# Fewer TensorE tiling changes, two weight loads swapped, and batch-1 transposes moved ahead of the last scale rows, in a one-core MM-DiT block

## The chip, the cores and the metric

The kernel runs on one core of one Trainium2 chip. The metric is the device time of one execution in microseconds (us). Before the change it was 120.38 us (three runs, 120.31 to 120.49). Two lengths occur below. The **time** is what the device reports for an execution. The **span** is what the trace covers, from the first to the last recorded instruction of the core.

## The reference

A joint attention block with image and text tokens (2 batches, 256 image and 32 text tokens, width D = 1152, bf16). Cut to what matters:

```python
mod_i = (silu(c) @ wmod_img).reshape(B, 6, 1, D)          # rows: shift, scale, gate, ... for the image
mod_t = (silu(c) @ wmod_txt).reshape(B, 6, 1, D)          # the same for the text
hi = layernorm(x_img) * (1 + sci) + shi                   # image tokens, scaled and shifted
ht = layernorm(x_txt) * (1 + sct) + sht
qi, ki, vi = split(hi @ wqkv_img);  qt, kt, vt = split(ht @ wqkv_txt)
q, k, v = concat(qt, qi), concat(kt, ki), concat(vt, vi)  # per batch: 32 text + 256 image tokens
a = softmax(q @ k.T * D ** -0.5) @ v
out_i = x_img + gai * (a[:, Nt:] @ wo_img)
out_t = x_txt + gat * (a[:, :Nt] @ wo_txt)
```

## The kernel before: the parts that the change touches

Twelve weight blocks of 1152 x 1152 pass through five SBUF slots. The loads of one queue are issued in order, and a load into a slot waits until the last reader of what was in it is done.

```python
w_sc_t = load_w(1, wmod_txt, D)            # text scale weights, slot 1
w_q_t = load_w(2, wqkv_txt, 0)
w_k_t = load_w(3, wqkv_txt, D)
w_v_t = load_w(1, wqkv_txt, 2 * D)         # text values: slot 1, after the text scale weights
w_ga_i = load_w(0, wmod_img, 2 * D)        # image gate: slot 0
w_ga_t = load_w(2, wmod_txt, 2 * D)
w_o_i = load_rows(3, wo_img, 0)
w_o_t = load_rows(1, wo_txt, 0)
```

A product with the two conditioning rows is made with four column tiles of 32 (tiling 128*32, set by `tile_position`), nearly all other large matmuls of the body with the full array (128*128); the text values and a few transposes have tilings of their own. In the head, the image scale rows end in one PSUM tile of 288 columns, which VectorE transposes at once, scales the first image columns with, and so opens the value matmuls:

```python
def mod_cols_of(gps, name):                # one VectorE transpose of [128, 9 x 32]
    t = const.tile([P, KT, LW], f32, ...)
    pin(nc.vector.transpose(t[:].rearrange("p c l -> p (c l)"), gps[:].rearrange("p c l -> p (c l)")))
    return t
...
sc_rows(0, 4)
warm_up(3)
sc_rows(4, 7)
warm_up(1)
out01 = x_transposes(0, 1)                 # six batch-1 transposes of 128x128
sc_rows(7, K8)
sc_rows(K8, KT)                            # the last scale rows to arrive
out31 = x_transposes(3, 1)
sc1_i = mod_cols_of(sc_ps, "scc")
out01()
x_scale(0, 3, 0)
out61 = x_transposes(6, 1)
v_open(A0, 0, 3)                           # the value matmuls begin
```

The places where the tiling changes in the body, the text rows, the scores, the softmax transposes and the text values:

```python
def txt_transposes():                      # nine transposes in 64-row tiling
    tpt = ps_tr.tile([P, KT, NTT], bf, tag="tr")
    for kt in range(KT):
        tr(tpt[:, kt, :], xn_t[:, kt * P:(kt + 1) * P], ident[0:NTT, 0:NTT])
    nc.scalar.copy(xT_t[:], tpt[:])
...
qk_img(w_k_i, 1, {1: (txt_shift_split, txt_rows_scale,),
                  6: (txt_rows_shift, txt_cols_shift, txt_modulate),
                  8: (lambda: qk_txt(0, w_q_t),)})
...
def attn_pair(ids0, ids1):                 # six full tiles of three feature blocks, cut
    ...
    for n, key in enumerate([x for pair in zip(t0, t1) for x in pair]):
        first = key in t1
        r0, (b, dt) = 64 * (n % 2), key    # two row tiles of 64
        mm((t1 if first else t0)[key][:], lhsT=v_t[r0:r0 + 64, dt * P:(dt + 1) * P],
           rhs=pTs[b][r0:r0 + 64, 2, :], start=first, stop=not first, tile_position=(r0, 0))
    ...
scores_txt()                               # 32-column tiles
scores_img(0)                              # full tiles
img_gate()                                 # 32-column tiles
scores_img(1)
v_txt()
p_transposes(0)                            # per batch: six full and three 32x32 transposes
txt_gate()
G = [[(b, dt) for dt in range(d0, d0 + 3)] for b in range(B) for d0 in range(0, KT, 3)]
attn_pair(G[0], G[1])
p_transposes(1)
attn_pair(G[2], G[3])
attn_pair(G[4], G[5])
```

## Time and profile before

| | before |
|---|---|
| time, median (range) of 4 runs | 120.34 us (120.27 to 120.49) |
| span of the profiled run | 118.6 us |
| time minus span | 1.8 us |
| TensorE (PE) busy | 112.1 us, 95% |
| first value matmul | 14.76 us |
| from there to the end of the span | 103.85 us |

The page of the profiled run gives busy time for each engine. The chain of waits follows the work that ended last back to the start, and names at each step what released it. In the chain a line is: start in us, length in us, engine, tile, source line, number of instructions. Line 61 is the helper through which every matmul goes, line 64 the one for transposes, so one has to go by the tile's name: `vps` are the image values, `gps` rows of scale, shift or gate, `sps` scores, `aps` attention, `pT_ps` softmax transposes, `ps` the other projections.

The prediction shows the head of this chain. Its part from 54 us on, cut, is what parts 3 to 6 of the change are about:

```profile
55.03 1.22 PE gps L61 x36
...
66.07 0.60 PE gps L61 x16
...
77.33 3.14 PE sps L61 x36
80.47 1.22 PE gps L61 x36
...
86.57 0.61 PE pT_ps L64 x9
...
90.55 0.50 PE pT_ps L64 x9
91.05 4.38 PE aps L61 x36
```

The text scale rows (36 `gps`) and shift rows (16 `gps`) are 11 us apart. The scores of text and of batch 0 are one entry of 36 matmuls and the image gate's 36 rows follow; the text scores come first there, so the 128*32 stays on both sides of the image scores are separate. The softmax transposes are in two places. No step in this stretch names another engine or a load: PE runs from one group to the next.

### The profile page before, as it was taken

How to read it: one execution, taken by the hardware profiler on the slowest of the kernel's cores; microseconds unless marked ns; L12 is line 12 of the kernel's file. 1: busy time of each engine (PE TensorE's matmuls, PEld its weight loads, DVE VectorE, ACT ScalarE, POOL GpSimd, SP SyncE). 2: the span in 40 equal slices, each digit the busy share in tenths (PEclk: the TensorE clock that was granted, in tenths of full speed). 3: DMA queues.
4: the chain of work that ended last, by engine and by line, in shares of the span. 5: the costliest groups of instructions: out<-in, count | busy, mean ns of one | idle time of the engine just before them, and what ended most of it. 6: DMA issues, size and time to landing. Idle time of an engine off the chain costs nothing.

```text
span 118.6 us, 2515 instructions
## 1 busy us (share of the span) xinstructions
PE 112.1 (95%) x1051; PEld 64.0 (54%) x1059; DVE 75.3 (63%) x157; ACT 41.8 (35%) x86; POOL 10.3 (9%) x31
## 2 busy tenths in 40 slices
PE   4988899999999999999999999999999999999990
PEld 1335544445674444445444457877876666666660
DVE  2568592063966799999999540048685666666571
ACT  4799620041752524323039233345327620000000
POOL 7110000000000000000000000000409017000000
PEclk9999999999999999999999999999999999999998
DMA  4999999999999999999999999999999996220223
GB/s 104 382 392 399 404 410 406 413 412 411 411 389 384 413 412 410 405 413 411 412 413 412 410 407 413 412 404 412 405 408 411 412 389 219 109 89 16 99 50 100
DMA packets 18613, 40.86 MB, mean 345 GB/s; under 512 B 1019, under 2 KB 1547, under 8 KB 18603
## 3 DMA queue, kind: packets, MB, share of 16 engines
q1 hardware_dynamic: 17728, 39.56, 85.7%
q0 software_dynamic: 480, 0.89, 2.2%
q10 hardware_dynamic: 395, 0.26, 0.7%
q8 instruction: 8, 0.13, 0.4%
q14 instruction: 2, 0.02, 0.0%
HBM read 39.38 MB, written 1.34 MB: 343 GB/s over the span
## 4 chain that ended last, share of the span: by engine, by line
PE 86%; DMA 8%; DVE 2%; SPq 1%; issue 1%; DVEq 0%
PE ps L61 52%; PE vps L61 15%; DMA t<-in_wmod_img_dram 8%; PE gps L61 6%; PE aps L61 6%; PE sps L61 5%; PE sc_ps L61 1%; PE pT_ps L64 1%; SPq L104 1%; DVE tmp L629 1%; DVE o L630 0%; DVE scc L217 0%; SPq L108 0%; PE tpt L64 0%; PE tp L64 0%
## 5 line engine op out<-in xcount | busy, mean ns | idle before, releaser
L61 PE MATMUL ps<-xT_i,t 128*128 128x512 bf16 x157 | 35.6, 380 | 0.3
L61 PEld LDWEIGHTS <-t 128*128 128x128 bf16 x324 | 20.4, 98 | 19.2 <-issue 0.7
L395 DVE SCALAR_TENSOR_TENSOR acc_sh<-t,sTf,acc_sh 128x1152 f32<-128x1152 bf16 x16 | 21.3, 1404 | 0.0
L61 PE MATMUL ps<-t,aT 128*128 128x384 bf16 (+3 forms) x153 | 20.2, 308 | 0.0
L61 PE MATMUL vps<-t,hS_i 128*128 128x512 bf16 (+1 forms) x106 | 17.8, 325 | 0.3 <-DVE hS_i L248 0.2
L61 PEld LDWEIGHTS <-aT 128*128 128x128 bf16 (+1 forms) x153 | 13.0, 101 | 7.1 <-issue 0.5
L61 PEld LDWEIGHTS <-hS_i 128*128 128x128 bf16 x108 | 9.0, 98 | 8.8 <-DVE hS_i L248 0.3
L629 DVE TENSOR_TENSOR tmp<-ps,gb 128x384 bf16<-128x384 f32 (+2 forms) x13 | 6.8, 526 | 6.3 <-PE ps L61 6.3
L346 ACT ACTIVATE qkT<-ps 128x512 bf16<-128x512 f32 (+2 forms) x11 | 6.2, 561 | 12.1 <-PE ps L61 12.1
L61 PE MATMUL wps<-warm 128*128 128x512 bf16 x25 | 7.7, 458 | 1.6 <-DVE unit L132 1.5
L481 POOL DMA_DIRECT2D mod_scratch<-g_sb x4 | 2.5, 634 | 76.6 <-ACT g_sb L174 76.6
L348 ACT CAST qkT<-ps 128x512 bf16<-128x512 f32 (+2 forms) x11 | 5.9, 554 | 8.3 <-PE ps L61 8.3
L172 DVE CAST v_i<-vps 128x512 bf16<-128x512 f32 x5 | 3.5, 692 | 8.2 <-PE vps L61 8.2
L553 DVE TENSOR_TENSOR half<-sps,half 64x288 f32<-64x288 f32 x1 | 0.4, 448 | 9.0 <-ACT half L552 9.0
L587 DVE TENSOR_SCALAR aT<-aps,svc 128x288 bf16<-128x288 f32 x9 | 4.5, 518 | 2.6 <-PE aps L61 2.5
L61 PEld LDWEIGHTS <-sT 128*32 128x32 bf16 x180 | 4.5, 96 | 2.8 <-issue 2.2
L174 ACT CAST v_i<-vps 128x512 bf16<-128x512 f32 x4 | 2.3, 580 | 10.0 <-PE vps L61 10.0
L61 PE MATMUL sps<-qkT 128*128 128x288 bf16 (+1 forms) x54 | 5.6, 288 | 0.0
L61 PEld LDWEIGHTS <-warm 128*128 128x128 bf16 x26 | 2.6, 111 | 5.2 <-issue 2.1
L61 PE MATMUL aps<-pT,v_i 128*128 128x288 bf16 x36 | 5.3, 288 | 0.0
L589 ACT ACTIVATE aT<-aps,svc 128x288 bf16<-128x288 f32 x9 | 4.1, 498 | 3.0 <-PE aps L61 2.9
L61 PE MATMUL gps<-t,sT 128*32 128x288 bf16 x144 | 5.1, 287 | 0.0
(104 smaller groups left out, 108.0 us busy)
## 6 DMA issues: line engine op xcount, KB each, us to landing
t<-in_wqkv_txt_dram SPq DMA_DIRECT2D x3, 2592.0 KB, 16.5
t<-in_wmod_img_dram SPq DMA_DIRECT2D x2, 2592.0 KB, 13.9
t<-in_wqkv_img_dram SPq DMA_DIRECT2D x2, 2592.0 KB, 20.1
t<-in_wmod_txt_dram SPq DMA_DIRECT2D x2, 2592.0 KB, 15.5
t<-in_wmod_txt_dram SPq DMA_DIRECT2D x3, 864.0 KB, 14.7
t<-in_wo_img_dram SPq DMA_DIRECT2D x3, 864.0 KB, 12.3
t<-in_wo_txt_dram SPq DMA_DIRECT2D x3, 864.0 KB, 11.4
t<-in_wqkv_img_dram SPq DMA_DIRECT2D x3, 576.0 KB, 9.2
```

Of the source, the lines that this page charges most:

```text
L61: return pin(nc.tensor.matmul(*a, **k))
L64: return pin(nc.tensor.transpose(*a, **k))
L104: nc.sync.dma_start(x_i[:, b * TPB:(b + 1) * TPB, :], x_img[b].rearrange("(p t) d -> p t d", t=TPB))
L172: nc.vector.tensor_copy(out_ap, in_ap)
L174: nc.scalar.copy(out_ap, in_ap)
L346: nc.scalar.mul(out_ap, in_ap, SCALE)
L348: nc.scalar.copy(out_ap, in_ap)
L395: pin(eng.scalar_tensor_tensor(acc[:, b, :], w[:, kt, :], sTf[:, kt, b:b + 1], acc[:, b, :], op0=ALU.mult, op1=ALU.add))
L481: nc.gpsimd.dma_start(gsc[si, b, :].rearrange("(g j) -> g j", g=NGG), g_sb[b:P:32, :])
L587: nc.vector.tensor_scalar(dst, tiles[(b, dt)][:], bias, None, op0=ALU.add)
L589: nc.scalar.activation(dst, tiles[(b, dt)][:], ACT.Identity, bias=bias)
L629: nc.vector.tensor_mul(tmp[:, 0:n], ps[:, 0:n], gb[:, b, c0:c0 + n])
```

## The change

The intent is to take PE out of and back into another tiling as rarely as possible, because each such excursion costs PE time, and to shorten the serial piece between the last scale rows and the first value matmul. (A run of matmuls in another tiling is called a stay; going there and coming back, an excursion.) In seven parts, as the prediction numbers them: (1) the head: scale columns in three pieces, a first scale of one token tile, and 12 batch-1 transposes ahead of the last scale rows; (2) text transposes in full tiles; (3) text scale rows next to the text shift rows; (4) image scores of batch 0 ahead of the text scores; (5) both softmax transposes together and full; (6) text values in four row tiles of 32; (7) the loads of image gate and text values swapped.

```diff
-    w_v_t = load_w(1, wqkv_txt, 2 * D)
     w_ga_i = load_w(0, wmod_img, 2 * D)
+    w_v_t = load_w(1, wqkv_txt, 2 * D)
@@ the head
+    def sc_cols(c0, c1):
+        pin(nc.vector.transpose(sc1_i[:, c0:c1, :]..., sc_ps[:, c0:c1, :]...))
-    A0 = [(0, 0), (1, 0), (0, 1), (1, 1)]
+    A0 = [(0, 0), (0, 1), (1, 0), (1, 1)]
     sc_rows(4, 7)
-    warm_up(1)
     out01 = x_transposes(0, 1)
+    out31 = x_transposes(3, 1)
     sc_rows(7, K8)
     sc_rows(K8, KT)
-    out31 = x_transposes(3, 1)
-    sc1_i = mod_cols_of(sc_ps, "scc")
+    out61 = x_transposes(6, 1)
     out01()
-    x_scale(0, 3, 0)
-    out61 = x_transposes(6, 1)
+    sc_cols(0, 1)
+    x_scale(0, 1, 0, step=1)
+    sc_cols(1, 5)
+    x_scale(1, 3, 0)
     v_open(A0, 0, 3)
     out31()
     out61()
+    x_scale(0, 3, 1)
+    sc_cols(5, KT)
@@ text transposes: two halves of the columns stacked on the partitions
-        for kt in range(KT):
-            tr(tpt[:, kt, :], xn_t[:, kt * P:(kt + 1) * P], ident[0:NTT, 0:NTT])
+        for k in range(KH):
+            tr(tpt[:, k].rearrange("p h t -> p (h t)"), xn_t[:, k * P:(k + 1) * P], ident[:])
@@ text scale rows
-    qk_img(w_k_i, 1, {1: (txt_shift_split, txt_rows_scale,),
-                      6: (txt_rows_shift, txt_cols_shift, txt_modulate),
+    qk_img(w_k_i, 1, {1: (txt_shift_split,),
+                      6: (txt_rows_scale, txt_rows_shift, txt_cols_shift, txt_modulate),
@@ softmax transposes: the text rows of the second batch through a rotated identity
-            tr(pT_ps[:, kj, qp:qp + NT], pb[r0:r0 + NT, kj * P:(kj + 1) * P], ident[r0:r0 + NT, r0:r0 + NT])
+            if b:
+                one(kj, pbs["t"], qpos[b][2], ident2)
+            for qi in range(TPB):
+                one(kj, pbs[(b, qi)], qpos[b][qi], ident)
+            if not b:
+                one(kj, pbs["t"], qpos[b][2], ident)
@@ text values
-            r0, (b, dt) = 64 * (n % 2), key
-            mm(..., lhsT=v_t[r0:r0 + 64, dt * P:(dt + 1) * P], rhs=pTs[b][r0:r0 + 64, 2, :], ...)
+            r0 = 64 * (n // 2 % 2) + NT * b
+            mm(..., lhsT=v_t[r0:r0 + NT, dt * P:(dt + 1) * P], rhs=pTs[b][r0:r0 + NT, 2, :], ...)
@@ order of the attention
-    scores_txt()
     scores_img(0)
+    scores_txt()
     img_gate()
     scores_img(1)
     v_txt()
     p_transposes(0)
+    p_transposes(1)
     txt_gate()
-    G = [[(b, dt) for dt in range(d0, d0 + 3)] for b in range(B) for d0 in range(0, KT, 3)]
-    attn_pair(G[0], G[1])
-    p_transposes(1)
-    attn_pair(G[2], G[3])
-    attn_pair(G[4], G[5])
+    for d0 in range(0, KT, 3):
+        attn_pair(*[[(b, dt) for dt in range(d0, d0 + 3)] for b in range(B)])
```

Cut are the allocation of the padded tiles, whose GpSimd memsets moved to the start, the second identity, and the two halves of the text norm.

## The prediction

> **What bounds the kernel now.** I read the page first: busy shares, then the chain that ended last by engine, because a 95% busy engine is only the bound if the chain also runs along it.
>
> ```profile
> PE 112.1 (95%) x1051; PEld 64.0 (54%) x1059; DVE 75.3 (63%) x157; ACT 41.8 (35%) x86; POOL 10.3 (9%) x31
> PE 86%; DMA 8%; DVE 2%; SPq 1%; issue 1%; DVEq 0%
> ```
>
> TensorE (PE) holds 86% of the chain, and DMA 8%, all of it at the start. Next I read the chain in order of time, at both ends of the DMA part.
>
> ```profile
> 2.12 9.85 DMA t<-in_wmod_img_dram
> ...
> 13.47 0.33 PE sc_ps L61 x4
> 13.80 0.02 issue
> 13.83 0.49 DVE scc L217
> ...
> 14.42 0.30 DVE hS_i L248
> 14.72 0.05 issue
> 14.76 2.12 PE vps L61 x9
> ```
>
> So there are two regimes. Until 13.47 us the load of the image scale weights sets the time; from the last scale rows to the first value matmul there is a serial piece, matmul, VectorE transpose (0.49), scale (0.30), of 1.29 us. From 14.76 on PE runs on. I checked this by counting: 63 value matmuls of 512 columns should take 63 x 0.216 = 13.61 us, and from the first of them to the next kind of matmul it is 13.70 us. The 0.09 us left over is the next thing to look at. PE's timeline, in narrow windows, shows where such remainders lie (columns: start, us; a group's start is its first matmul):
>
> ```profile
> 54.65 0.38 PE L61 MATMUL ps<-xT_i,t 128*128 128x512 bf16 x1
> 54.96 0.30 PE L61 MATMUL gps<-t,sT 128*32 128x288 bf16 x3
> ...
> 55.95 0.30 PE L61 MATMUL gps<-t,sT 128*32 128x288 bf16 x4
> 56.18 0.39 PE L61 MATMUL ps<-xT_i,t 128*128 128x512 bf16 x1
> ```
>
> Matmuls of 512 columns normally start 0.216 apart; ahead of the first 128*32 one it is 0.31, so **entering another tiling costs 0.094**. Four-at-a-time groups of 288 columns start 0.122 apart (36 of 288 in nine groups); after the last one it is 0.219-0.23, so leaving costs about 0.107, and the first interval after each change is 0.010 longer. An excursion and its return cost 0.094 + 0.107 + 2 x 0.010, about **0.22 us** of pure PE time. PE being the bound, each excursion removed after 14.76 us should come off the end.
>
> **What the Trainium skill says.** "TensorEngine Tiling (Array Packing)", Key Properties: changing the tiling mode, not just the tile, drains TensorE. The trace agrees; the drain is the 0.1 us above. "TensorE: Matmul & The Clock Gate", Measured speedup vs the span model: concurrent tiles add about 4 ns each, and four row tiles with K=32 gave 3.07 times. The trace shows the 4 ns for column tiles and for two row tiles; four row tiles are in no run yet. "VectorE: DVE Perf Modes", the TRN2 errata: small VectorE operations from SBUF pay a fixed cost each. The trace agrees: a scale of 256 columns takes 0.286, one of 1152 takes 0.576, so a line of 0.20 + 0.335 per 1000 columns. "Trainium Kernel Development and Optimization", NeuronCore Architecture: VectorE runs at 0.96 GHz. The trace has no second size of the same transpose to test that rate with; I use it for one estimate.
>
> **The change part by part.**
>
> 1. Head. The scale columns are transposed in three pieces (32, 128, 128 columns), the first scale is cut to one token tile, and 12 batch-1 transposes fill the wait for the last rows in place of one warm-up matmul and 6 of them. The last rows still arrive at 13.43, so their matmuls stay at 13.475. The transpose of 288 columns took 0.483; at one column a cycle, 288/0.96 GHz is 0.30, leaving a fixed 0.18, so 32 columns take about 0.216 (estimate with the clock of that page): 0.267 saved. The 128-wide scale is about 0.237 instead of 0.286: 0.05 saved. The next k-row must be scaled by its turn, four matmuls (0.86) later: the second scale, a 128-column transpose (0.32) and a 256-wide scale end about 15.21 against 15.31, close but in time. The first rows of the value weights landed at 14.14 and 14.85, in time for starts of 14.45 and 15.31. Only six transposes remain after the last rows; they wait for a copy that ends near 13.85 and are over near 14.2. **-0.32**.
>
> 2. Text transposes: nine in 64-row tiling become five full ones.
>
> ```profile
> 46.41 0.38 PE L61 MATMUL ps<-xT_i,t 128*128 128x512 bf16 x1
> 46.72 0.43 PE L64 MATMUL tpt<-ident,xn_t 64*128 64x64 bf16 x9
> 47.09 0.39 PE L61 MATMUL ps<-xT_i,t 128*128 128x512 bf16 x1
> ```
>
> From the matmul before to the second one after is 0.309 + 0.366 + 0.227 = 0.90; full transposes start 0.056 apart, so it becomes 0.216 + 0.28 + 0.216 = 0.71. **-0.19**. The extra VectorE and ScalarE instruction lies beside PE.
>
> 3. The text scale rows (36 matmuls) move next to the shift rows (16 matmuls), one excursion fewer: **-0.22**. Their last shift part must be ready: VectorE finished it at 65.44; it is needed about 65.65 in the new order.
>
> 4. Image scores of batch 0 go ahead of the text scores, so that these and the gate rows, both 128*32, are one stay: **-0.22**. In the old order the text scores also had one gap of 0.21 between groups instead of 0.11, waiting for the last text keys; nine image-score matmuls come in between now: **-0.10**.
>
> 5. Both softmax transposes stand together as 18 full ones; the text rows no longer use 32-row tiling. Old: 0.605 + 0.60 (start to start) plus 0.01; new: 18 x 0.056 + 0.10 = 1.11. **-0.10**.
>
> 6. Text values in attention: six matmuls of 64 rows in three pairs become four and two of 32 rows.
>
> ```profile
> 88.70 0.53 PE L61 MATMUL aps<-pT,v_i 128*128 128x288 bf16 x3
> 89.17 0.54 PE L61 MATMUL aps<-pT,v_t 64*128 64x288 bf16 x6
> 89.64 0.67 PE L61 MATMUL aps<-pT,v_i 128*128 128x288 bf16 x4
> ```
>
> The stay is 0.475 long, pairs 0.12 apart; two groups instead of three saves 0.12, in each of three pairs: **-0.36**. It has 0.65 in the middle pair, since the second batch's probabilities were still being copied by ScalarE (0.878, to 91.97); with both transposes earlier that copy hides under the gate rows: **-0.17**.
>
> 7. Loads. The image gate block landed about 79.2 and is used at 80.40: the smallest margin of the late loads, and less than parts 1 to 4 gain. Swapped, it takes the place that landed at 72.8, and the text values take the later one (79.3), needed about 82.9. So the swap earns nothing by itself but keeps this load from becoming the new wait. The other loads are queued behind others and should land as before: text gate 85.7 for 86.5, output weights 87.9 to 92.2 from 93.5.
>
> Sum: 0.32 + 0.19 + 0.22 + 0.32 + 0.10 + 0.53 = **1.68 us**, all on PE's path or ahead of it. 120.38 - 1.68 = 118.70.
>
> **The rivals.** (a) **A load becomes the bound.** DMA moves over 400 GB/s nearly all the way to 95 us, and PE moves ahead of it by up to 1.7 us. For: the text gate has only about 0.8 us left. Against: by the landing times every late load keeps some margin. If one binds, 0.3 to 0.8 is given back: 119.0 to 119.5. (b) **Evacuation binds in attention.** A pair takes PE about 1.92 instead of 2.06 (0.84 + 0.475 + 0.745); six evacuations of 0.4 to 0.49 on two engines need 1.47. For: the third buffer is free only about 0.05 to 0.1 before its turn. Against: it is enough on paper. If it binds, up to 0.3 is lost: 119.0. (c) **The gate's round trip** through DRAM: issue at 83.0, landing at 95.5, first multiply at 96.93, which moves to about 95.3. Against: ScalarE copies the gate earlier (it stood behind two exponentials), so the landing moves too, near 94; and PSUM buffers cover some delay. Result unchanged. (d) **The head gains nothing**, because the second k-row comes late: 0.05 to 0.2 lost, 118.9. (e) **Four row tiles overlap badly**: 0.36 lost, 119.06.
>
> **Range and chances.** The small parts are counted from intervals that repeat to 0.005, so the sum is good to about 0.2 if nothing new waits; the rivals pull one way, later. I take 118.70 with 118.3 to 119.4. Faster by over 2% would need below 117.97, 0.7 more than all parts give: 0.05. Slower by 2% would need a stall of 4 us, which nothing shows: 0.01.
>
> **What would show it.** First value matmul at about 14.45; no 64*128 and no 32x32 matmuls; a 128*32 stay of 52 matmuls near 64, one of 54 near 79.5; text-value stays of about 0.355 three times; out matmuls starting about 93.6; and gaps of single matmuls only at tiling changes. It would be wrong if PE shows a wait on a DMA after 14 us, on an attention evacuation, or if the 32-row stays take 0.475 or more.

## The result, and the profile after

Both kernels were correct. Executions over 1.5% slower than the fastest of the same kernel are left out of the means. Ratios here and below are the mean time of one kernel's fast runs over that of the other's of the same rounds, so they are not quite the ratio of the medians.

| | before | after |
|---|---|---|
| time, median (range), 4 runs each | 120.34 (120.27 to 120.49) | 119.28 (118.96 to 119.55) |
| ratio | | 0.9909 (95%: 0.9882 to 0.9936) |
| span of the profiled run | 118.6 | 116.8 |
| time minus span | 1.8 | 2.1 to 2.16 |
| first value matmul | 14.76 | 14.40 |
| from there to the end | 103.85 | 102.44 |

The kernel got faster by 0.9%. The traced span of the profiled run fell by 1.8, a little more than the 1.68 foretold, but the time of that run (118.96) is the lowest of its four. Part of what the span gained is not in the time: the difference between the two grew from 1.8 to 2.1.

The page's first part and the chain by engine of the changed kernel (busy us, share of the span, number of instructions; then shares of the chain):

```profile
PE 110.7 (95%) x1046; PEld 63.7 (54%) x1054; DVE 75.7 (65%) x161; ACT 41.7 (36%) x87; POOL 11.2 (10%) x34
PE 85%; ACT 6%; DMA 4%; DVE 1%; issue 1%; DVEq 0%
```

PE's busy time fell by 1.4, VectorE (DVE) has four instructions more. In the chain the share of DMA halved and 6% of ScalarE (ACT) came in. The chain in order of time says where, and shows the later groups as they stand now:

```profile
0.74 4.18 DMA x_i<-in_x_img_dram
...
11.66 0.70 ACT xT_i L254
...
12.40 0.96 PE tp L64 x12
13.35 0.39 PE sc_ps L61 x8
...
14.40 2.12 PE vps L61 x9
...
64.18 1.71 PE gps L61 x52
...
76.55 2.92 PE sps L61 x36
79.47 1.10 PE gps L61 x36
...
85.46 1.11 PE pT_ps L64 x18
...
87.79 5.88 PE aps L61 x54
93.67 19.52 PE ps L61 x144
```

From 64 us on this is what was meant: one stay of 52 scale and shift rows, 18 softmax transposes in 1.11, and one entry of 54 attention matmuls where there were two with a transposes group between them. In the head the chain is another one. It starts at the load of x, not at the scale weights, goes through the layer norm and a copy out of PSUM on ScalarE (11.66 to 12.36), and the last 8 scale-row matmuls start at 13.35 behind 12 transposes although the last scale rows had landed at 12.97.

PE's timeline in narrow windows, changed kernel (start, length, engine, line, operation, tile and operands, tiling, shape, count):

```profile
46.26 0.44 PE L64 MATMUL tpt<-ident,xn_t 128*128 128x128 bf16 x5
46.54 0.38 PE L61 MATMUL ps<-xT_i,t 128*128 128x512 bf16 x1
...
88.56 0.42 PE L61 MATMUL aps<-pT,v_t 32*128 32x288 bf16 x6
88.91 0.66 PE L61 MATMUL aps<-pT,v_i 128*128 128x288 bf16 x4
```

Five transposes take 0.28 from start to start (46.26 to 46.54), as predicted, and the stay of six 32-row matmuls takes 0.35 (88.56 to 88.91), where the prediction had 0.355.

### The profile page after: what moved, and what is told of

Its sections match the earlier page's. It is cut to its first block, busy times and chain, and to the rows that moved or that the text cites. A ratio compares the mean times of both kernels' runs of the same rounds, so it can differ in the third digit from the quotient of the medians.

```text
span 116.8 us, 2512 instructions
## 1 busy us (share of the span) xinstructions
PE 110.7 (95%) x1046; PEld 63.7 (54%) x1054; DVE 75.7 (65%) x161; ACT 41.7 (36%) x87; POOL 11.2 (10%) x34
## 4 chain that ended last, share of the span: by engine, by line
PE 85%; ACT 6%; DMA 4%; DVE 1%; issue 1%; DVEq 0%
PE ps L61 53%; PE vps L61 15%; PE gps L61 6%; PE aps L61 5%; PE sps L61 4%; DMA x_i<-in_x_img_dram 4%; ACT xn_i L202 2%; ACT xn_i L201 2%; PE pT_ps L64 1%; PE tp L64 1%; ACT rstd L211 1%; ACT rstd L212 1%; ACT xT_i L254 1%; DVE tmp L650 1%; DVE o L651 0%
## 5 line engine op out<-in xcount | busy, mean ns | idle before, releaser
L542 DVE TENSOR_REDUCE nmx<-sps 128x1 f32<-128x288 f32 x4 | 1.7, 450 | 8.9 <-PE sps L61 8.9
L61 PE MATMUL ps<-hT_t,t 128*128 128x64 bf16 x162 | 5.1, 193 | 0.0
```

The source lines that it names most:

```text
L61: return pin(nc.tensor.matmul(*a, **k))
```

## The experiments

Twelve experiments were run: the changed kernel once more, and eleven variants of it. Two theories stood at the start. **A, the tiling account**: parts 2 to 6 are worth 1.36 us of PE time, the sum that the prediction made of intervals. **B, the head**: its gain is there or not by whether the last scale rows or the image tokens come last. The rivals to these were a cost outside the trace (**C**, tied to the number of VectorE instructions) and a standing-still of PE at instruction transfers (**D**), which came up when traces with equal programs differed. Single start times below are those of matmuls in the traces. The accounts use the length from the first value matmul to the end of the span ("body"), which leaves the head out. Where the expectations count VectorE's instructions they count two more than the profile's page does; the text below keeps to the page's count, 157 before and 161 after.

### The same kernel again

No edit: the changed kernel, with more runs, to see how far equal programs differ.

> The changed kernel unaltered, on another occasion, to see whether the first profile was typical. Theory A (sum of PE parts): span 1.7 to 1.8 us below that of the kernel before in every run, median time about 1.1 to 1.7 us below it. Theory B (the head is no longer bound by the last scale rows but by the image path, layer norm on ScalarE and then twelve transposes): the first value matmul again near 14.4 us or later, and the spread of the runs larger than that of the kernel before (0.2 us).

Measured: 119.53 us (118.93 to 119.72), ratio 0.9923 (0.9894 to 0.9953); a sixth run, at 120.73 (its clock was 0.999), is left out. Neither expectation came true. The median is 0.76 below the kernel before, less than theory A's 1.1. Of theory B's signs, the first value matmul came at 14.20, not 14.4 or later, and the spread (118.93 to 119.72) is no larger than that of the kernel before in the same rounds (119.96 to 120.72, 11 runs). The profiled run's trace has a body of 103.18, not 102.44. PE's timeline shows one of the two places where it stood still (columns as above, then idle time and what ended it):

```profile
74.90 0.28 PE L61 MATMUL ps<-hT_t,t 128*128 128x64 bf16 x4 [0.21 <-issue]
```

The bracket says that PE sat idle for 0.21 before the group, and what ended it: "issue", so nothing that the profile shows. By the start times of single matmuls two of them are 0.377 further apart than their neighbours, and two others near 80.5 us 0.353. Without these two the body is 102.45. So the body repeats to 0.01 us, and an addition comes and goes.

### The head undone

```diff
-    A0 = [(0, 0), (0, 1), (1, 0), (1, 1)]
+    A0 = [(0, 0), (1, 0), (0, 1), (1, 1)]
     sc_rows(4, 7)
+    warm_up(1)
     out01 = x_transposes(0, 1)
-    out31 = x_transposes(3, 1)
     ...
-    sc_cols(0, 1)
-    x_scale(0, 1, 0, step=1)
-    sc_cols(1, 5)
-    x_scale(1, 3, 0)
+    sc_cols(0, KT)
+    x_scale(0, 3, 0)
```

> The changed kernel with the old head: one warm-up matmul, six batch-1 transposes ahead of the last scale rows, one transpose of all scale columns, scales of 256 columns, old order of the value matmuls. Theory A: 0.32 us slower than the changed kernel, first value matmul near 14.76. Theory B: the head's gain is lost whenever the weights land early, since then the image path decides; difference 0 to 0.15 us, and possibly none in time.

Measured: **118.81 us** (118.69 to 119.05), ratio 0.988 (0.9858 to 0.9901). Without the new head the kernel is no slower; its median is lower than that of the changed kernel, where theory A had it slower by 0.32 and theory B by 0 to 0.15. Body 102.47, so parts 2 to 6 are whole. Its head, in the chain in order of time, has the one transpose of 288 columns back:

```profile
13.60 0.50 DVE scc L261
```

From the landing of the last rows (13.20) to the first value matmul it takes 1.33, as in the kernel before (13.43 to 14.76). Its profiled run has a span of 117.0, no shorter than those of the changed kernel. But its time minus its span is 1.79 to 1.85 in all runs, not 2.1. What the head saves inside the span, something takes back outside it. The page counts 158 VectorE instructions here, three fewer than with the new head. That is theory C.

### Six transposes in the wait instead of twelve

```diff
     out01 = x_transposes(0, 1)
-    out31 = x_transposes(3, 1)
     sc_rows(7, K8)
     sc_rows(K8, KT)
+    out31 = x_transposes(3, 1)
     out61 = x_transposes(6, 1)
```

> The changed kernel with its scale columns in three parts, but only six batch-1 transposes ahead of the last scale rows and twelve after them. Theory B: the last scale rows start about 0.3 us earlier where they have landed (13.0 instead of 13.3 to 13.4), first value matmul near 14.1, time 0.1 to 0.3 us below the changed kernel. Theory A (the load of the last rows decides): no difference, or 0.05 us slower since twelve transposes stand after the rows.

Measured: 119.23 us (118.67 to 119.78), ratio 0.9909 (0.988 to 0.9938), not to be told from the changed kernel by time. The trace tells more. The last rows landed at 13.07 and the first value matmul started at 14.11, 1.04 later; the changed kernel took 1.43 for a landing at 12.97.

```profile
3.73 9.34 DMA t<-in_wmod_img_dram
13.11 0.31 PE sc_ps L61 x4
13.42 0.78 PE tp L64 x12
```

The chain begins at the scale weights again and the scale-row matmuls start 0.04 after the landing: no transposes stand ahead of them. The other twelve run between the scale rows and the values, while VectorE transposes and scales. Body 102.44.

### Text values in 64 rows

```diff
-            r0 = 64 * (n // 2 % 2) + NT * b
-            mm(..., lhsT=v_t[r0:r0 + NT, ...], rhs=pTs[b][r0:r0 + NT, 2, :], ...)
+            r0 = 64 * (n % 2)
+            mm(..., lhsT=v_t[r0:r0 + 64, ...], rhs=pTs[b][r0:r0 + 64, 2, :], ...)
```

> The changed kernel with the text values of attention as six matmuls of 64 rows again. Theory A: three stays of 0.475 instead of 0.35 us, 0.36 to 0.38 us slower in span and time. Rival (evacuation decides in attention): less than 0.1 us slower, the stays longer but the gaps after them shorter.

Measured: 119.88 us (119.36 to 120.16), ratio 0.9961 (0.9936 to 0.9987). PE's timeline:

```profile
89.28 0.54 PE L61 MATMUL aps<-pT,v_t 64*128 64x288 bf16 x6
89.76 0.42 PE L61 MATMUL aps<-pT,v_i 128*128 128x288 bf16 x2
```

A stay of 0.48 (89.28 to 89.76) against 0.35 with four row tiles. The body is 103.19, of which one standing-still is 0.353; the rest, 102.84, is 0.40 above 102.44. The prediction had 0.36 for three pairs. In this run the last rows landed late, at 13.72, and the first value matmul came 1.03 later: when the scale rows bind, the new head does save 0.30.

### The swap undone

```diff
-    w_ga_i = load_w(0, wmod_img, 2 * D)
     w_v_t = load_w(1, wqkv_txt, 2 * D)
+    w_ga_i = load_w(0, wmod_img, 2 * D)
```

> The changed kernel with the loads of the image gate and of the text values in the old order. By the prediction the image gate block then lands near 79.3 and is wanted near 79.2: a wait of PE on this load of 0.1 to 0.3 us in the trace, median 0.1 to 0.3 us above the changed kernel. If the first value matmul comes late in the profiled run (after 14.7), the wait vanishes. Rival: no wait at all, the swap is worth nothing.

Measured: **123.54 us** (123.41 to 124.09), ratio 1.0274 (1.025 to 1.0299), with a span of 121.3 to 121.9. This is by far the largest effect, and no theory had it. The chain in order of time:

```profile
65.92 16.33 DMA t<-in_wmod_img_dram
...
82.30 2.22 PE gps L61 x36
84.52 3.00 PE sps L61 x18
```

The gate load was issued at 65.92 and landed at 82.25; the gate rows, which run at 79.47 in the changed kernel, started 3.08 us after the matmul before them; the list of waits counts 2.8 us of that as idle.

Why so late? The text values go into slot 1, which the text scale weights hold until their last reader. In the kernel before that was at 55 to 56 us, and the load of the text values was issued at 56.3. Part 3 of the change moved the scale rows to 64.2, so slot 1 came free only at 65.4. The queue is in order. The gate load, whose slot 0 had long been free (62.7 in the changed kernel), stood behind it. The list of waits of the issuing queue shows the one wait, 11.8 us, on the scale rows' matmuls (us, times, longest):

```profile
SPq L89 <- PE gps L61: 11.8, 1, 11.8
```

The queue had nothing left to move meanwhile. The DMA view of 66 to 73 us, first with the swap undone, then of the changed kernel:

```profile
DMA packets 1025, 2.37 MB, mean 339 GB/s; under 512 B 1, under 2 KB 1, under 8 KB 1024
```

```profile
DMA packets 1247, 2.85 MB, mean 407 GB/s; under 512 B 17, under 2 KB 17, under 8 KB 1246
```

That is 0.48 MB less in this window alone. The wait had a second cost. Busy times of the window 82 to 86 us (its length; PE, weight load, VectorE, ScalarE, GpSimd, each with its count; then granted clock, DMA share, GB/s):

```profile
82.00:86.00 4.00, 3.70 (x43) 2.24 (x44) 0.90 (x4) 0.69 (x3) 0.74 (x1) 0.57 1.05 415
```

After that stretch the granted clock was 0.5 from 82.5 to 85.9. By the start times of single matmuls, the gate rows took 2.16 instead of 1.32 and the 18 scores 3.00 instead of 2.31: 1.5 us more. (The chain's entries of 2.22 and 1.10 for the gate rows can't be compared: in the changed kernel the entry begins only when the matmuls before have ended, by which time several gate rows have started.) The wait of 3.08, the 1.52 of the lower clock and a small gap of 0.10 near 74.8 us make up the whole difference of the bodies, 107.14 against 102.44. The Trainium skill has this: "TensorE: Matmul & The Clock Gate", Why this matters for your kernels, warns of PE-idle gaps of more than about 3 us between bursts of matmuls, because the clock falls back to half. This run agrees, at a gap of 3.08 from start to start; where the limit lies, one gap can't show.

### The old head with three more VectorE instructions

The old head of the second experiment, with its memset of a small constant cut in four. The three added instructions run at the very start; PE's first warm-up matmul starts 0.08 us later for them (1.57 against 1.49), and the rest of the head does not wait for it.

```diff
-    nc.vector.memset(eps_row[:], EPS)
+    for q in range(4):
+        nc.vector.memset(eps_row[:, 8 * q:8 * q + 8], EPS)
```

> The kernel with the old head, with one small memset of VectorE at the very start cut into four, so that VectorE has as many instructions as in the changed kernel (163 instead of 160). The time of a run is longer than the span of its records by 1.8 us in the kernel before and with the old head, by 2.1 us wherever the new head is in. Theory C (the 0.3 us outside the span comes with the number of VectorE instructions): time minus span 2.1 us here, span unchanged near 117.0, so median 119.1. Rival (it comes with something else in the new head): time minus span 1.8 us, median 118.8.

Measured: 119.17 us (118.47 to 119.8), ratio 0.9911 (0.9876 to 0.9945). Spans are 116.4 to 117.7, with a median of 117.05, as for the head undone; but time minus span is 2.07 to 2.13 in every run instead of 1.79 to 1.85. Body 102.45. The page counts 161 VectorE instructions.

### The new head with three fewer VectorE instructions

Two memsets and a small copy go to GpSimd, which has time.

```diff
-    nc.vector.memset(eps_row[:], EPS)
+    nc.gpsimd.memset(eps_row[:], EPS)
-    nc.vector.memset(unit[:], 1.0 / P)
+    nc.gpsimd.memset(unit[:], 1.0 / P)          # placed a few lines later
-    nc.vector.tensor_copy(shT32[:, :, 0:B], sh_i[:, :, 0:B])
+    nc.gpsimd.tensor_copy(shT32[:, :, 0:B], sh_i[:, :, 0:B])
```

> The changed kernel with three small VectorE instructions (two memsets, one copy of 18 columns) moved to GpSimd: 160 VectorE instructions. Theory C: time minus span 1.8 us instead of 2.1, spans spread as in the changed kernel (116.8 to 117.6), median about 119.0. Rival: time minus span stays 2.1, median 119.3.

Measured: **118.76 us** (118.48 to 119.76), ratio 0.9884 (0.9852 to 0.9915). Time minus span is 1.76 to 1.85 in every run. So the difference goes with the number of VectorE instructions and not with the head, tested both ways (here GpSimd got the three instructions; in the run before, nothing else changed). The trace is of its slowest run (span 118.0): the last rows landed at 14.09, the latest of all traces, and the values began 1.03 later, at 15.12; one standing-still of 0.35 came on top.

### The instructions shifted by 64 and by 144

Theory D: PE stands still at certain instructions because the transfer that brings the next ones is late. The two places are 257 records apart in the trace, and an instruction transfer moves 16384 bytes. If the place hangs on the count of instructions, more short warm-up matmuls at the start move it to other matmuls.

```diff
-    warm_up(14)
+    warm_up(12)                                  # by 64 PE instructions; by 144: 6 and 80
+    for _ in range(34):
+        mm(wps[:, 0:64], lhsT=warm[:, 0:P], rhs=warm[:, 0:64], start=True, stop=True)
```

> The changed kernel with 2 warm-up matmuls replaced by 34 tiny ones in the idle time before the first transposes: 64 more PE instructions ahead of all others. In two traces of the changed head PE stood still for 0.36 to 0.41 us with no semaphore to wait for, 257 records apart, 1.3 to 1.5 us after an instruction transfer of 16384 bytes had landed. Theory D (PE runs dry of instructions: a block of 256 is asked for when the one before it is entered, and arrives about 6.1 us later while weights load; the changed order uses 256 instructions in 5.9 us): the block limits move by 64 instructions to places where 256 last 7 us, no stall in the trace, spans near 116.8 with less spread, median about 118.9. Rival (the stalls have another cause): spans 116.8 to 117.6 as before.

> As the run with 64 more PE instructions, but 144 more (80 tiny matmuls for 8 warm-up ones). Theory D: one block now falls on the text queries and keys, where 256 instructions last only about 5.4 us; PE stalls about 0.7 us at the start of the image scores (near 76 us) in the trace and in nearly all runs; spans 117.4 or more. Rival: no difference from the run with 64 more.

Measured: 119.36 us (119.01 to 119.99), ratio 0.9924 (0.9896 to 0.9951), and 119.29 us (119.14 to 119.44), ratio 0.9918 (0.9898 to 0.9938). Neither trace shows a standing-still at the old places, but each is one trace, and half of those of the unshifted programs show none either. The first has a spread of times (0.98) no smaller than the unshifted kernel's, and in the second the stall expected near 76 us did not come: its body is 102.46, and its six times lie within 0.30, with a median no lower. The first has a gap of 0.12 near 94 us whose cause was not found. The numbers of theory D are refuted; what is left of it stands in the section on the prediction.

### Six transposes in the wait and three fewer VectorE instructions

Both edits at once, as the best version that the experiments pointed to.

> The version that the runs so far point to: the changed kernel with only six transposes ahead of the last scale rows and with 160 VectorE instructions. Expected: first value matmul 1.03 to 1.05 us after the landing of the last scale rows whether these land early or late; from there to the end 102.4 us plus 0.36 where PE stalls; time minus span 1.8; median about 118.5, against 119.3 of the changed kernel. If theory C or the image path were not the causes, it would be no faster than the changed kernel.

Measured: 119.08 us (118.62 to 119.46), ratio 0.9891 (0.9867 to 0.9915); time minus span 1.76 to 1.85 as expected. The trace has a body of 103.11 with both places of standing still, about 0.30 and 0.35. Its head took 1.03 from a landing at 13.51, late enough that an early landing was not tested. The 118.5 expected was missed. It is not to be told from either single step (119.23 and 118.76); what it can win in the head is less than what the standing-still alone added in this trace.

### The stays kept apart

Parts 3 and 4 undone: the text scale rows back to their old place, text scores ahead of the image scores.

```diff
-    qk_img(w_k_i, 1, {1: (txt_shift_split,),
-                      6: (txt_rows_scale, txt_rows_shift, txt_cols_shift, txt_modulate),
+    qk_img(w_k_i, 1, {1: (txt_shift_split, txt_rows_scale,),
+                      6: (txt_rows_shift, txt_cols_shift, txt_modulate),
...
-    scores_img(0)
     scores_txt()
+    scores_img(0)
```

> The changed kernel with the text scale rows and the text scores where they were (parts 3 and 4 of the prediction undone): two more excursions into 128*32 tiling, and the wait for the last text keys back. From the first value matmul to the end 102.44 + 0.54 = 102.98 us in the trace. Rival: the excursions were partly hidden, less than 0.3 us more.

Measured: 119.73 us (119.44 to 120.03), ratio 0.9945 (0.9924 to 0.9966). The chain in order of time has the scale rows back at 54.86 by themselves, and the 36 scores of text and batch 0 in 3.14 instead of 2.92:

```profile
54.86 1.22 PE gps L61 x36
...
77.17 3.14 PE sps L61 x36
```

Body 103.04, 0.60 more than 102.44. Two small gaps of 0.015 and 0.028 lie at the places of standing still; without them it is 0.56. The prediction had 0.22 + 0.22 + 0.10 = 0.54.

### The transposes as before

Parts 2 and 5 undone: nine text transposes in 64-row tiling, and softmax transposes with 32x32 pieces for the text, but both batches still together. Two text instructions and the second norm go with it.

```diff
-        for k in range(KH):
-            tr(tpt[:, k].rearrange("p h t -> p (h t)"), xn_t[:, k * P:(k + 1) * P], ident[:])
+        for kt in range(KT):
+            tr(tpt[:, kt, :], xn_t[:, kt * P:(kt + 1) * P], ident[0:NTT, 0:NTT])
...
+        for kj in range(3):
+            tr(pT_ps[:, kj, qp:qp + NT], pb[r0:r0 + NT, ...], ident[r0:r0 + NT, r0:r0 + NT])
```

> The changed kernel with the text transposes in 64-row tiling and the text rows of the softmax transposes in 32-row tiling (parts 2 and 5 undone). From the first value matmul to the end 102.44 + 0.19 + 0.10 = 102.73 us in the trace. Rival: the full transposes cost as much as they save, no difference.

Measured: 119.31 us (119.27 to 119.36), ratio 0.9914 (0.9896 to 0.9932). Body 102.76, 0.32 more than 102.44; predicted 0.19 + 0.10 = 0.29. The text transposes are again nine in 64*128 in PE's timeline, and the softmax's 18 take 1.22 instead of 1.11 in the chain in order of time:

```profile
85.82 1.22 PE pT_ps L64 x18
```

By time this run is level with the changed kernel, and yet its body is longer; it has one VectorE instruction fewer (160), and time minus span is 1.98 to 2.07, between the two groups above.

## Why the prediction was right or wrong

The class (within 2%) and the range (118.3 to 119.4) held; the point, 118.70, was 0.6 us too low. The Trainium skill's statement that the prediction rests on, "TensorEngine Tiling (Array Packing)", Key Properties, that a change of tiling mode drains TensorE, agrees with the one run that undoes joined stays and hardly anything else: with the stays kept apart the body is 0.56 to 0.60 longer. That a change costs time is shown; that a drain is the reason rests on the page.

| part | predicted | measured, by undoing |
|---|---|---|
| 2 + 5, transposes | 0.29 | 0.32 |
| 3 + 4, stays joined | 0.54 | 0.60, or 0.56 without two small gaps |
| 6, text values in 32 rows | 0.36 | 0.40 |
| 6, wait in the middle pair | 0.17 | not undone by itself |
| sum of 2 to 6, body | 1.36 | 103.85 - 102.44 = 1.41 |
| 1, head | 0.32 | 0.30 if the scale rows come last; less or nothing if not; nothing in the mean span of all runs |
| 7, swap | 0 | about 4.3 of time, as 123.54 against 119.28; 4.7 of the body |
| outside the span | not considered | a loss of 0.3 |

**Parts 2 to 6 were right, in mechanism and in size.** The body shrank by 1.41 where 1.36 was foretold; the undone parts and the unmeasured 0.17 add to 1.45 with the lower figure for the stays, to 1.49 with the higher. Joining excursions is worth what intervals of single matmuls say, since PE is the only chain there.

**Part 1: the step that failed is "the last rows still arrive at 13.43", and with it that 12 transposes "fill the wait".** The head's three pieces are right: where the rows bind, the way from landing to the first value matmul fell from 1.33 to 1.03 in seven traces, and single pieces measured as estimated (32 columns 0.216, 128 columns 0.308 for 0.32, the 128-wide scale 0.25 for 0.237, where the prediction's own line of 0.20 + 0.335 per 1000 would give 0.243). The clock of 0.96 GHz that the prediction took from the Trainium skill for the size of a transpose fits: 96 columns more cost 0.092 us, 160 more 0.175, so 0.96 to 1.1 ns a column, where that clock ("Trainium Kernel Development and Optimization", NeuronCore Architecture) gives an estimate of 1.04. But the landing is not a constant. Over the traces it lies between 12.80 and 14.09. The 12 transposes wait themselves, for ScalarE's copy of earlier ones out of PSUM that ends at 12.36, so they hold PE until 13.35, and rows that land before then wait for them. In the two traces where they landed at 12.80 and 12.97 the way took 1.40 and 1.43: longer than in the old head. Six transposes in the wait cured this in the trace (1.04 for a landing at 13.07), but its worth, at most 0.4 in some runs, is below what the times can tell. So it was luck that the first value matmul of the first trace came at 14.40, next to the 14.45 foretold: the rows landed 0.46 earlier than assumed, and the way from there took 0.41 longer than the new head's 1.02.

**Part 7: the step that failed is "So the swap earns nothing by itself".** The rest of that sentence, that it keeps the load from becoming the new wait, was right in direction, but the size was missed by far: 4.3 us, and not the 0.1 to 0.3 that was expected of undoing it. The working took the landing time of before, 79.2, for the gate. That held only if the loads were issued as before, and part 3 of the same change moved the release of slot 1 from 56 to 65 us. Rival (a), a load that becomes the bound, was thus the strongest of the rivals, and the swap is why it did not come. That a swap put in for a margin of a few tenths saved this much was luck. The change as made has the text values behind the gate, issued at 65.4, and no PE wait in the body names a load.

**Rivals (b), (c), (d) and (e) did not come.** There was no wait on an evacuation in attention; the gate's round trip landed at 94.1 and 95.4 for the two batches, with output matmuls from 93.67 on and no wait for it on the chain; the second k-row of the values was in time; four row tiles ran their six matmuls in 0.35. Of the four row tiles, of which the prediction said that no run had them yet, the matmuls start 3 to 4 ns apart.

**What the prediction did not see.** First, 0.3 us outside the span. Time minus span is 1.8 with 157 or 158 VectorE instructions, 2.0 with 160 and 2.1 with 161, and it followed the number when that was changed without the head, in both directions. This is shown; what the device does in that time is not, as nothing outside the span is recorded. Nor do these counts tell a cost of each instruction from a limit that is crossed: 157 and 158 do not differ. Three of the four added instructions belong to the new head, two more pieces of transpose and one more scale; the fourth is the second half of the text norm. Inside the span the new head saves 0.3 at best, and the spans show none of it: their means are 117.0 and 117.1 in the two kernels with the old head, and 117.1 to 117.3 in the seven sets of runs with the new head and the rest of the body as changed. Outside the span it costs 0.3. So undoing it (118.81) loses nothing. Second, two places where PE stands still with nothing in the trace that it waits for. Of the fourteen traces, four show it at one place or both, 0.30 to 0.38 each time, and two more show 0.02 to 0.10 there. In those six the 16384-byte instruction transfers start at 72.5 to 73.1 and 78.5 to 79.1; in the six others whose PE program was not shifted at 67.5 to 68.8 and 76.9 to 77.4, and these have no such gap. So lateness of the transfer goes with the standing still. What makes a transfer late is open, and the shifted programs, with one trace each, do not settle it.

The 0.6 us of the miss then has two terms. One is the 0.3 outside the span, which is shown. The other is the 0.3 of the head: the mean span fell from 118.5 (that of the kernel before, in later rounds) to 117.1, which is the body's 1.4 and no more. Why the head's 0.3 is missing from the spans is shown only for the traces with early landings; landings and standing still vary from run to run (spans of 116.8 to 117.4 for the same program), and the runs without a trace do not tell them apart.

The best versions measured are the changed kernel with three VectorE instructions moved to GpSimd (118.76) and the one with its old head (118.81). Both beat the kernel before, by 1.2% of its time, and have lower medians than the kernel as changed; their intervals overlap with its own.

## What to carry to other kernels

Count tiling changes on a PE-bound path: each excursion cost about 0.22 us here, and joining stays gave what was computed. When a group of matmuls moves, ask which buffer it is the last reader of, and which loads stand behind the load into that buffer in the same queue: here a reordering that saves 0.22 would have cost 4.3 us without a swap of two lines. Compare the time with the span for every version: a gain inside the trace can be lost outside of it, and moving a few small instructions to an idle engine can bring it back.

## What the Trainium skill lacked or had wrong

- "TensorEngine Tiling (Array Packing)", Key Properties, says that a mode change drains TensorE and gives no cost. Here entering another tiling cost 0.094 us, leaving it 0.107, an excursion and return 0.22.
- "Runtime: NRT & Kernel Launch", Instruction fetch mechanics, calls the crossing of a 16 KiB block of instructions "mostly hidden". In four of fourteen traces PE stood still for 0.30 to 0.38 us at one or both of two places 257 records apart, and in two more a little; these are the traces in which the 16384-byte transfers started late. That the transfers are the cause is not shown.
- None of the pages read tells of the time outside the recorded span growing with the length of one engine's program: 1.8 us with 157 or 158 VectorE instructions, 2.1 with 161.
- "VectorE: DVE Perf Modes", The TRN2 errata, gives 120 + FD/Accel cycles for VectorE operations that read PSUM. For a transpose of 32, 128 and 288 float32 columns, at one column a cycle and the page's 0.96 GHz, that is an estimate of 0.158, 0.258 and 0.425 us; here they took 0.216, 0.308 and 0.483. The growth per column agrees, the fixed part is 0.05 to 0.06 larger.
